# Windowed attention ahead of a SiLU MLP on one core: early transposes ahead of products, V's scale finished inside the MLP, and a ring of four parts for the statistics

## The chip, the cores and the metric

The kernel runs on one core of a Trainium2 chip. The metric is the device time of one execution in microseconds (us). The engines are named as in the profile: PE is TensorE (matmuls; PEld its weight loads), DVE is VectorE, ACT is ScalarE, POOL is GpSimd, SP is SyncE, which here issues every DMA. Each engine works through its own queue in order.

## The reference

```python
def _attn_ref(q, k, v):                       # (8, 8, 576, 64): batch, heads, sequence, width
    scores = scale * np.matmul(q, k.transpose(0, 1, 3, 2))
    bias = slopes[:, None, None] * (-np.abs(rel))[None]
    mask = (rel >= 0) & (rel < 128)           # a causal window of 128
    scores = np.where(mask, scores + bias[None], -1000000000.0)
    attn = np.exp(scores - np.max(scores, axis=-1, keepdims=True))
    attn = attn / (np.sum(attn, axis=-1, keepdims=True) + 1e-09)
    return np.matmul(attn, v)

def _moe_ref(x, w_in, w_out):                 # x: 4608 x 512, w_in: 512 x 2048, w_out: 2048 x 512
    h = x @ w_in
    return (h * (1.0 / (1.0 + np.exp(-h)))) @ w_out
```

The attention's result, heads put side by side, is the x of the MLP. Both run in one launch.

## The kernel before

**Blocks and pairs.** The 4608 rows are 36 blocks of 128 rows. A block has eight heads; four of them are one *pair* p = 2i + q (block i, half q), so there are 72 pairs. Two batches of the reference make one batch b of the kernel: four of them, nine blocks each. The MLP takes groups g of four blocks (512 rows), nine groups, and each group runs 16 slices f of the hidden width; n = 16 g + f counts slices over the whole program.

**An order written out by hand.** Nothing is scheduled by the compiler. The MLP's matmuls are a fixed sequence of *points*, numbered from 0: `gemm1(n, half)` and `gemm2(n, half)`, one half each, 64 points to a group. Everything else is put at a point by `put(point, function, ...)` and is recorded just ahead of that point's matmuls; what stands at the same point keeps the order in which it was put. Points below 0 are the *early part*, which has no matmuls of the MLP: there the attention of the first eight pairs (`p < 2 * GT`) runs alone, in steps of eight points. `at(p)` is the point of pair p's scores: `STEP * (p - 8) - 18` for the first eight, the list `CLOSE` for the next eight, then one every eight points.

**A pair.** `scores` (L431, L424): q times k into two PSUM banks. `row_max` (L453): bias and row maximum, on DVE. `exps` (L463): on ACT. For the first eight pairs `p_transpose_first` (L495) transposes the weights on PE and `p_copy_first` copies them out of PSUM, half 0 on ACT (L504), half 1 on DVE (L502); later pairs go through `p_hi`, `p_lo` (L472, L477) and a DMA transpose (L485). `attend` (L514, L527) is the product with V; `normalize` (L540 to L554) divides, on DVE, and frees the PSUM bank. During the MLP the scores of a pair take both banks of tag "a", one of which is that of the `attend` two pairs earlier, so they wait for that pair's `normalize`. `x_transpose`/`x_low` (L579 to L584) make the first group's x.

**V.** V is split into two 16-bit parts, `v_hi` on POOL (L400) and `v_lo` on DVE (L406), with a power-of-two scale per batch. That scale comes from `vscale_load` (a DMA of one block of V), `vscale_reduce` (its absolute maximum) for each of nine blocks, and `vscale_finish` in three stages: a maximum on DVE (L233), a transpose on PE (L237) with five small instructions on DVE, and a broadcast on PE (L247) with a copy (L249). From batch `QK16 = 2` on, q and k get such statistics too: `qk_load` (L202) fetches q and k of a block, `qk_sum` (L212) sums their absolute values on ACT in place.

**The weights.** They are loaded as raw 64-bit words (`w_load`, L720 and L725) and split by `w_next`: two instructions on ACT (L730, L737), one on DVE (`w_join`, L742), one on ACT (`w_hi`, L752) and one on POOL (`w_lo`, L135). Each of 32 slices is split once, some in the early part, the rest during group 0.

**The MLP's chain.** After `gemm1(n)`: `act1` on ACT (gt, L647), `act2` on DVE (L652), `act3` on ACT (gh, L660 or L662), `act4` (gl; on POOL at L135 in groups 0 to 2 but for the last slice, then on DVE). `gemm2(n)` needs gh for its first two matmuls and gl for the third. At the end of a group `turn_over` does these at once.

**DMA waits.** SP's DMAs use eight semaphores in turn. SP stops at a DMA until what it overwrites is free, and everything behind it in SP's queue stops too.

Of the kernel before, what the change touches and what calls it, by code (L numbers as in the profile page):

```python
# [6 lines left out]
F32 = mybir.dt.float32  # L7
# [5 lines left out]
AF = mybir.ActivationFunctionType  # L13
# [4 lines left out]
P = 128  # L18
B, H, S, D = 8, 8, 576, 64
NHP = H // 2  # L20
DM, DFF = 512, 2048
# [3 lines left out]
NBLK = SB // P  # L25
# [7 lines left out]
GT = TG // P  # L33
NF = DFF // P
NCC = DM // P
# [19 lines left out]

IN16, OUT16 = 2, 3
QK16 = 2
STATS16 = ("w1_10", "w1_11")
RAW16 = ("w1_0", "w1_1")
Q16 = ("w1_2", "w1_3")  # L60
K16 = ("w1_4", "w1_5", "w1_6")
# [9 lines left out]
KEPT = 6  # L71
WD = (1, 2, 3)

CLOSE = (1, 5, 8, 14, 20, 26, 32, 38)


def at(p):

    if p < 2 * GT:
        return STEP * (p - 2 * GT) - 18  # L80
    if p < 4 * GT:
        return CLOSE[p - 2 * GT]
    return STEP * (p - 2 * GT) - LEAD
# [3 lines left out]
def tile_window_attention_then_silu_mlp(ctx, tc, qk, qk16, v, w_in, w_out, base8, out):  # L87
# [35 lines left out]
    def early_tile(i):  # L123
        return early_part(i // 2, i % 2)
# [49 lines left out]

    def vscale_load(b, i):

        t = early_tile(i) if b == 0 else pool.tile([P, DM], F32, tag="rv", bufs=2, name=f"vm{b}_{i}")
        nc.sync.dma_start(t, v[b, i * P : (i + 1) * P, :])
        vred.setdefault(b, {})[i] = t = t.rearrange("p (h d) -> p h d", h=H)
        if b == 0 and i < KEPT:  # L180
            rvs[i] = t

    def vscale_reduce(b, i):
# [6 lines left out]
        else:  # L190
            junk = pool.tile([P, H, D], F32, tag="gt", name=f"vj{b}_{i}")
            nc.scalar.activation(junk, t, AF.Abs, accum_out=m)

    def qk_load(b, i):

        if b == QK16:
            if i == 0:
                vred[b, "qk"] = pool.tile([P, 4, DM], F32, tag="xl", bufs=1, name=f"qs{b}")
            t = vred[b, "qk"][:, 2 * (i % 2) : 2 * (i % 2) + 2]
        else:  # L200
            t = pool.tile([P, 2, DM], F32, tag=STATS16[i % 2], bufs=1, name=f"qs{b}_{i}")
        nc.sync.dma_start(  # L202
            t.rearrange("p k (h c) -> p k h c", h=NHP), qk[b * NBLK + i].rearrange("k p h c -> p k h c")
        )
        vred[b, "qk", i] = t

    def qk_sum(b, i):

        t = vred.pop((b, "qk", i))
        for k in range(2):  # L210
            m = vred[b]["m"][:, (1 + k) * VCH + i : (1 + k) * VCH + i + 1]
            nc.scalar.activation(t[:, k], t[:, k], AF.Abs, accum_out=m)  # L212

    wsc = {}

# [367 lines left out]
    def x_low(cc):  # L583
        nc.vector.tensor_sub(xl[:, cc], xps.pop(cc), f32(xh[:, cc]))  # L584
# [219 lines left out]
    def put(point, fn, *a):  # L804
        plan.setdefault(max(point, at(0)), []).append((fn, a))

    for p in range(NPAIR):
        i, q = divmod(p, 2)
        n = at(p)
        if p < 2 * GT:  # L810
            a = n + 2 * STEP + 1
        elif p == 2 * GT:
            a = n + 10
        elif p == 2 * GT + 1:
            a = n + 12
        else:
            a = n + (15 if p < 4 * GT else 13 if i < QK16 * NBLK else 12)
        if i >= QK16 * NBLK:
            put(n - 18, load_qk16, p)
            put(n - 10, hi16, p, 0)  # L820
            put(n - 8, hi16, p, 1)
            put(n - 6, lo16, p, 0)
            put(n - 5, lo16, p, 1)
            if block_of(i) == 0 and q == 0:
                put(n, rescale_bias, i // NBLK)
        put(n, scores, p)
        if block_of(i) in (SPLIT, SPLIT + 1):
            put(n + 1, other_batch, p)
        put(n + 1, row_max, p, 0)
        put(n + 1, row_max, p, 1)  # L830
        put(n + 2, exps, p, 0)
        put(n + 3, exps, p, 1)
        if p < 2 * GT:

            for u in range(2):
                put(n + STEP + 3, p_transpose_first, p, u)
                put(n + STEP + 4, p_copy_first, p, u)
        else:
            put(n + 3, p_hi, p, 0)
            put(n + 4, p_lo, p, 0)  # L840
            put(n + 4, p_hi, p, 1)
            put(n + 4, p_transpose, p, 0)
            put(n + 5, p_lo, p, 1)
            put(n + 5, p_transpose, p, 1)
        put(a, attend, p)
        z = a + 1
        put(z, normalize, p, 0)
        put(z + 1, normalize, p, 1)
        put(z + 2, x_hi, p)
        put(z + 2, x_lo, p)  # L850
        if q == 0:
            if 1 < i < QK16 * NBLK:
                put(at(2 * i - 3) + 1, load_q, i)
                put(at(2 * i - 3) + 1, load_k, i)
            if i >= KEPT:
                put(n + 4, load_v, i)
            if i == GT:
                put(a - 5, v_hi, i - 1)
                put(a - 4, v_lo, i - 1)
            if i >= GT:  # L860
                put(a - 3, v_hi, i)
                put(a - 2, v_lo, i)
    for k in range(2 * NF):
        put(STATS + k, w_stat, k % 2, k // 2)
    for x, wait in enumerate((0, 2, 5)):
# [3 lines left out]
            for k, fn in enumerate((conv1, conv2, conv3)):  # L869
                put(n + SLICE * f + (CLEAR if f > 4 else 0) + (k if which or f else 0), fn, which, f)  # L870
    for g in range(1, NG):
        put(at(2 * GT * g) + 10, x_unit, g)
        if g >= IN16:
            put(g * SLICE * NF - 2, mlp_scales, g)
    for b in range(1, NBB):

        n = at(2 * GT * (NBLK * b // GT)) + 2
        for i in range(VCH):
            put(n - 53 + 5 * i, vscale_load, b, i)
            put(n - 49 + 5 * i, vscale_reduce, b, i)  # L880
            if b >= QK16:
                put(n - 52 + 5 * i, qk_load, b, i)
                put(n - 46 + 5 * i, qk_sum, b, i)
        for x, wait in enumerate((0, 2, 5)):
            put(n + wait, vscale_finish, b, x)

# [27 lines left out]
    with tc.manual_schedule():  # L914
        make_identity(nc, ident)
        nc.gpsimd.memset(ones, 1.0)
        ps_of("a", "warm")
        keep_warm(16)

        warm = const.tile([P, 1], F32, name="warm")  # L920
        nc.scalar.activation(warm, ones[:, :1], AF.Exp)
        load_q(0)
        load_k(0)
        nc.sync.dma_start(tab[:, :, P:], base8[:, :, P:])
        load_whole(0)
        load_q(1)
        load_k(1)
        nc.sync.dma_start(tab[:, :, :P], base8[:, :, :P])
        load_whole(1)
        nc.gpsimd.memset(v1[:, :, :, D : D + 1], 1.0)  # L930
        for i in (2, 3):
            put(at(2 * i - 3) + 1, load_whole, i)
        for i in range(GT, VCH):
            put(at(4) + 3 + 3 * (i - GT), vscale_load, 0, i)
        for i in range(VCH):
            put(at(3) + 6 + 4 * i, vscale_reduce, 0, i)
        for x in range(3):
            put(at(7) + (6, 8, 16)[x], vscale_finish, 0, x)
        for n in range(AHEAD):
            put(at(1) + 4 + 5 * n, w_next_load)  # L940
        put(at(0) + 1, keep_warm, 6)
        put(at(1) + 1, keep_warm, 16)
        for n in (at(5) + 5, at(6) + 5, at(7) + 5):
            put(n, w_next)
        for cc in range(2):
            put(at(7) + 13 + cc, x_transpose, cc)
        put(at(7) + 14, x_low, 0)
        put(at(7) + 20, x_low, 1)
        while pos[0] < 0:
            begin()  # L950
            pos[0] += 1
        bank.update(scores=[("a", "a")])

        for g in range(NG):
            now[0] = g

            seq = []
            for f in range(NF):
                n = g * NF + f
                seq += [("g1", n, 0)] + [("xt", 0, 2), ("xt", 0, 3)] * (n == 0) + [("g1", n, 1)]  # L960
                if 0 < f < NF - 1:
                    seq += [("g2", n - 1, 0), ("g2", n - 1, 1)]
            n = g * NF + NF - 1
            seq += [("g2", n - 1, 0), ("g2", n - 1, 1), ("g2", n, 0), ("g2", n, 1)]
            for k, n, half in seq:
                if k == "xt":
                    x_transpose(half)
                    x_low(half)
                    continue
                begin()  # L970
                x_send()
                if k == "g1":
                    gemm1(n, half)
                    if half == 1:
                        act1(n)
                        if n % NF == NF - 1:
                            turn_over(n)
                        else:
                            later(1, act2, n)
                            later(2, act3, n)  # L980
                            later(2, act4, n)
                else:
                    gemm2(n, half)
                    if n % NF == NF - 1:
                        store(g, 2 * half)
                        store(g, 2 * half + 1)
                if g == 0 and half == (n == 0):
                    w_next()
                pos[0] += 1
        while plan:  # L990
            begin()
            pos[0] += 1
# [41 lines left out]
```

## Time and profile before

| what | us |
|---|---|
| runs of before: median, lowest, highest (3) | 952.33, 951.69, 953.88 |
| the profiled execution | 949.61 |
| its span in the trace | 947.8 |
| PE busy | 921.9 (97%) |
| DVE, ACT, POOL busy | 655.0, 558.9, 133.5 |

The profiled execution is the one whose trace is read here; 1.8 us of it lie outside the span. Matmuls are pipelined, so PE busy at 97% says that little time is left between matmuls, not that each runs at its best rate. In a row of the timeline stand: start and duration in us, engine, line, operation, output<-input, shape, how many alike were merged, and in square brackets the idle time of that engine just before, with what ended it. In a row of waits: who waited for whom, us in total, how many times, the longest.

### The profile page before, as it was taken

Reading aid. Unit: us, or ns where it says so; the run is one execution under the profiler, and the core shown is the slowest. Engines: PE = TensorE matmul, PEld = TensorE weight load, DVE = VectorE, ACT = ScalarE, POOL = GpSimd, SP = SyncE. Lnnn points to the kernel's source line nnn. Section 1 sums busy time; section 2 is a strip of 40 time slices with the busy share of each in tenths; the row PEclk is TensorE's granted clock in tenths of the full one; section 3 lists DMA queues with packets and bytes.
Section 4 is the critical chain, followed back from the end, with each engine's and each line's share of the span. In section 5 each row is a group of like instructions: output and inputs, shape, how many; then the busy total and the mean of one; then the engine's idle time right before and its main releaser. Section 6 shows DMA issues by size and latency. Waiting matters only on the chain.

```text
span 947.8 us, 17110 instructions
## 1 busy us (share of the span) xinstructions
PE 921.9 (97%) x6442; PEld 574.9 (61%) x6442; DVE 655.0 (69%) x1603; ACT 558.9 (59%) x1152; POOL 133.5 (14%) x122
## 2 busy tenths in 40 slices
PE   8799999999999999999999999999999999999998
PEld 7677777777778888555545555555555545554443
DVE  4687887555778887899687778776777777743222
ACT  5678888676555674666567756555655565532222
POOL 0145665121212221000000000000000000000000
PEclk9999999999999999999999999999999999999999
DMA  9949942423277762644597765544654554421001
GB/s 277 375 119 246 272 101 67 106 65 87 65 181 200 166 142 50 156 101 101 111 244 179 221 144 132 118 112 98 139 111 104 119 142 106 87 55 56 1 1 44
DMA packets 209266, 123.28 MB, mean 130 GB/s; under 512 B 172576, under 2 KB 180768, under 8 KB 209184
## 3 DMA queue, kind: packets, MB, share of 16 engines
q1 hardware_dynamic: 209184, 122.19, 51.9%
q8 instruction: 50, 0.82, 0.4%
q14 instruction: 32, 0.26, 0.1%
HBM read 72.35 MB, written 9.44 MB: 86 GB/s over the span
## 4 chain that ended last, share of the span: by engine, by line
PE 78%; ACT 5%; DVE 5%; issue 2%; DMA 1%; POOL 1%; SPq 0%; DVEq 0%; ACTq 0%; POOLq 0%
PE o L700 34%; PE h L634 29%; PE h L639 6%; PE av L527 4%; PE sp L424 3%; PE sp L431 2%; DVE wm L742 1%; ACT t L463 1%; DVE t L453 1%; DVE gt L652 1%; ACT gt L647 1%; DVE x L137 1%; ACT wr L737 1%; ACT hr L472 1%; DVE v L406 1%
## 5 line engine op out<-in xcount | busy, mean ns | idle before, releaser
L700 PE MATMUL o<-w,gh 128*128 128x512 f16 (+1 forms) x1152 | 351.2, 386 | 1.4 <-ACT gh L660 1.4
L634 PE MATMUL h<-xt,w 128*128 128x512 f16 (+1 forms) x1536 | 310.6, 353 | 0.0
L647 ACT ACTIVATE gt<-h,gsc 128x512 f32<-128x512 f32 x112 | 77.0, 688 | 259.9 <-PE h L634 257.6
L700 PE MATMUL o<-w,gl 128*128 128x512 f16 (+1 forms) x576 | 221.8, 385 | 2.7 <-POOL gl L135 1.5
L634 PEld LDWEIGHTS <-w 128*128 128x128 f16 x1536 | 144.5, 98 | 125.8 <-issue 2.2
L652 DVE SCALAR_TENSOR_TENSOR gt<-gt,h 128x512 f32<-128x512 f32 x144 | 98.6, 685 | 122.6 <-ACT gt L647 122.1
L700 PEld LDWEIGHTS <-gh 128*128 128x128 f16 x768 | 74.8, 98 | 88.7
L463 ACT ACTIVATE t<-t,mx 128x256 f32<-128x256 f32 (+1 forms) x288 | 121.2, 487 | 12.3 <-DVE mx L453 12.1
L477 DVE SCALAR_TENSOR_TENSOR hr<-t,hr 128x512 f16<-128x512 f32 (+1 forms) x128 | 94.6, 741 | 23.5 <-ACT hr L472 23.3
L668 DVE SCALAR_TENSOR_TENSOR gl<-gt,gh 128x512 f16<-128x512 f32 x96 | 66.4, 692 | 53.9 <-ACT gh L662 51.3
L639 PE MATMUL h<-xh,w 128*128 128x512 f32 x256 | 90.0, 405 | 0.0
L400 POOL TENSOR_SCALAR v<-rv,vsc 128x512 f16<-128x512 f32 x30 | 24.4, 814 | 446.1 <-DMA rv<-v 233.1
L135 POOL TENSOR_TENSOR gl<-gt,gh 128x512 fp32r<-128x512 f32 x45 | 60.2, 1337 | 189.0 <-ACT gh L660 154.7
L700 PEld LDWEIGHTS o<-w,gh 128*128 128x128 f32 x384 | 69.9, 188 | 16.6 <-ACT gh L660 1.8
L472 ACT ACTIVATE hr<-t 128x512 f16<-128x512 f32 (+1 forms) x128 | 76.3, 601 | 1.0 <-DMA hl<-hr 1.0
L662 ACT ACTIVATE gh<-gt 128x512 f16<-128x512 f32 x96 | 60.2, 627 | 22.1 <-DVE gt L652 20.9
L700 PEld LDWEIGHTS <-gl 128*128 128x128 f16 x384 | 37.5, 98 | 47.9 <-DVE gl L668 3.5
L527 PEld LDWEIGHTS <-hl 128*128 128x128 f16 x1464 | 51.8, 98 | 22.4 <-issue 13.0
L453 DVE CUSTOM_DVE_ANT_0 t<-sp,tab,vsc 128x256 f32<-128x256 f32 (+1 forms) x144 | 58.6, 463 | 9.2 <-PE sp L424 8.8
L527 PE MATMUL av<-v,hl 128*128 128x65 f16 (+1 forms) x1464 | 55.8, 193 | 7.1 <-DVE v L406 5.7
L137 DVE SCALAR_TENSOR_TENSOR x<-xs,x 128x256 f16<-128x256 f32 x64 | 43.9, 687 | 24.0 <-ACT x L564 23.7
L453 DVE CUSTOM_DVE_ANT_0 t<-sp,tab 128x256 f32<-128x256 f32 (+1 forms) x144 | 50.5, 401 | 13.4 <-DMA tab<-base 7.1
(130 smaller groups left out, 1026.4 us busy)
## 6 DMA issues: line engine op xcount, KB each, us to landing
r<-qk SPq DMA_DIRECT2D x36, 512.0 KB, 4.2
out<-ot SPq DMA_DIRECT2D x36, 256.0 KB, 2.5
qs<-qk SPq DMA_DIRECT2D x18, 512.0 KB, 5.7
wr<-w_in SPq DMA_DIRECT2D x16, 512.0 KB, 7.3
wr<-w_out SPq DMA_DIRECT2D x16, 512.0 KB, 6.8
rv<-v SPq DMA_DIRECT2D x30, 256.0 KB, 3.1
vm<-v SPq DMA_DIRECT2D x27, 256.0 KB, 4.1
q<-qk SPq DMA_DIRECT2D x18, 256.0 KB, 3.6
```

Of the source, the lines that this page charges most:

```text
L135: engine.tensor_sub(out, a, b)
L453: nc.vector.tensor_tensor_reduce(out=t[:, h, 2 * P - n :], in0=st[p]["sp"][h][:, u, o].rearrange("p o c -> p (o c)"), in1=tab[:, 4 * q + 2 ...
L463: nc.scalar.activation(x, x, AF.Exp, bias=st[p]["mx"][:, 2 * u + h : 2 * u + h + 1], scale=-1.0)
L472: nc.scalar.activation(split_of(p, u, hr)[:, 0], t[:, :, 2 * P - n :], AF.Copy, scale=PSCALE)
L477: nc.vector.scalar_tensor_tensor(out=hr[:, 1], in0=t[:, :, 2 * P - n :], scalar=PSCALE, in1=hr[:, 0], op0=ALU.mult, op1=ALU.subtract)
L527: nc.tensor.matmul(av[:, 2 * u + h, : rhs.shape[-1]], lhs, rhs, start=(n == 0), stop=(n == len(seq) - 1), skip_group_check=True,)
L634: nc.tensor.matmul(o, w[:, wp, cc], x, start=start and k == 0, stop=stop, skip_group_check=True)
L639: nc.tensor.matmul(hps[n], w[:, cc], x, start=(half == 0 and i == 0), stop=(half == 1 and i == len(seq) - 1), skip_group_check=True,)
L647: nc.scalar.activation(gt, hps[n], AF.Tanh, scale=scale)
L652: nc.vector.scalar_tensor_tensor(out=gt, in0=gt, scalar=1.0, in1=hps[n], op0=ALU.add, op1=ALU.mult)
L668: nc.vector.scalar_tensor_tensor(out=gl, in0=gt, scalar=CUT, in1=gh, op0=ALU.mult, op1=ALU.subtract)
L700: nc.tensor.matmul(ops[ti], a[:, t], w, start=(f == 0 and i == 0), stop=(f == NF - 1 and i == len(seq) - 1), skip_group_check=True,)
```

## The change

1. In the early part the transposes of a pair are put two points sooner and its product with V two points later (for pair 7: four points sooner), so that in each step PE does scores(p), transposes(p-1), product(p-2) where it did scores(p), product(p-2), transposes(p-1). The copies on ACT (half 0) now stand ahead of the next pair's exponentials.
2. V's scale of batch 0 is finished in the MLP: stage 0 at point -18, stage 1 (transpose) at point 1, stage 2 (broadcast) at point 4. It stood at -20, -18 and -10.
3. All four x transposes stand ahead of point 0; two stood inside the first `gemm1`. Pair 8's scores go to point -6 (`CLOSE[0]`), from 1.
4. Four weight slices instead of three are split ahead of the MLP, one in each step from pair 4 on, and none at point 1. The raw loads start six points later, V's block loads earlier.
5. `v_hi` and `v_lo` stand two points sooner throughout, and V's load three points sooner.
6. The statistics of later batches: for batch 1 the loads follow the list `VM1`. In batch 2, V, q and k of a block are three loads into the four parts of one tile, taken in turn (V of block i in part 3i mod 4, q in 3i + 1, k in 3i + 2); V had tiles of its own, and q and k of a block one 512 KB load into one of two halves. In batch 3 V, q and k have tiles of their own, two of each. The loads of block i stand at point n - 53 + 5i (q and k: one sooner), V's reduction at n - 48 + 5i (one later), the sums at n - 47 + 5i (one sooner).

```diff
-CLOSE = (1, 5, 8, 14, 20, 26, 32, 38)
+CLOSE = (-6, 5, 8, 14, 20, 26, 32, 38)
+VM1 = (-1, 3, 7, 11, 15, 19, 24, 32, 37)
...
-STATS16 = ("w1_10", "w1_11")
+STATS16 = (("w1_10", "w1_11"), ("w1_14", "w1_15"))
...
     def vscale_load(b, i):
-        t = early_tile(i) if b == 0 else pool.tile([P, DM], F32, tag="rv", bufs=2, name=f"vm{b}_{i}")
+        if b == 0:
+            t = early_tile(i)
+        elif b == QK16:
+            t = stat_parts(b)[:, 3 * i % 4]
+        else:
+            tag, bufs = ("rv", 2) if b == 1 else (("w1_12", "w1_13")[i % 2], 1)
+            t = pool.tile([P, DM], F32, tag=tag, bufs=bufs, name=f"vm{b}_{i}")
...
     def qk_load(b, i):
-        if b == QK16:
-            if i == 0:
-                vred[b, "qk"] = pool.tile([P, 4, DM], F32, tag="xl", bufs=1, name=f"qs{b}")
-            t = vred[b, "qk"][:, 2 * (i % 2) : 2 * (i % 2) + 2]
-        else:
-            t = pool.tile([P, 2, DM], F32, tag=STATS16[i % 2], bufs=1, name=f"qs{b}_{i}")
-        nc.sync.dma_start(t.rearrange(...), qk[b * NBLK + i].rearrange("k p h c -> p k h c"))
-        vred[b, "qk", i] = t
+        for k in range(2):
+            if b == QK16:
+                t = stat_parts(b)[:, (3 * i + 1 + k) % 4]
+            else:
+                t = pool.tile([P, DM], F32, tag=STATS16[k][i % 2], bufs=1, name=f"qs{b}_{i}_{k}")
+            nc.sync.dma_start(t.rearrange("p (h c) -> p h c", h=NHP), qk[b * NBLK + i, k])
+            vred[b, "qk", i, k] = t
...
-        if p < 2 * GT:
-            a = n + 2 * STEP + 1
+        if p == 2 * GT - 1:
+            a = n + 13
+        elif p < 2 * GT:
+            a = n + 2 * STEP + 3
         elif p == 2 * GT:
-            a = n + 10
+            a = n + 17
...
-                put(n + STEP + 3, p_transpose_first, p, u)
-                put(n + STEP + 4, p_copy_first, p, u)
+                put(n + STEP + 1, p_transpose_first, p, u)
+                put(n + STEP + 1 + u, p_copy_first, p, u)
...
-                put(n + 4, load_v, i)
+                put(n + 1, load_v, i)
             if i == GT:
-                put(a - 5, v_hi, i - 1)
-                put(a - 4, v_lo, i - 1)
+                put(a - 6, v_hi, i - 1)
+                put(a - 5, v_lo, i - 1)
             if i >= GT:
-                put(a - 3, v_hi, i)
-                put(a - 2, v_lo, i)
+                put(a - 5, v_hi, i)
+                put(a - 4, v_lo, i)
...
-        put(at(2 * GT * g) + 10, x_unit, g)
+        put(max(8, at(2 * GT * g) + 10), x_unit, g)
...
-            put(n - 53 + 5 * i, vscale_load, b, i)
-            put(n - 49 + 5 * i, vscale_reduce, b, i)
+            x = VM1[i] if b == 1 else n - 53 + 5 * i
+            put(x, vscale_load, b, i)
+            put(x + (4 if b == 1 else 5), vscale_reduce, b, i)
             if b >= QK16:
-                put(n - 52 + 5 * i, qk_load, b, i)
-                put(n - 46 + 5 * i, qk_sum, b, i)
+                put(n - 53 + 5 * i, qk_load, b, i)
+                put(n - 47 + 5 * i, qk_sum, b, i)
...
-            put(at(4) + 3 + 3 * (i - GT), vscale_load, 0, i)
+            put(at(2) + 4 + 5 * (i - GT), vscale_load, 0, i)
...
-            put(at(7) + (6, 8, 16)[x], vscale_finish, 0, x)
+            put((-18, 1, 4)[x], vscale_finish, 0, x)
         for n in range(AHEAD):
-            put(at(1) + 4 + 5 * n, w_next_load)
+            put(at(2) + 2 + 5 * n, w_next_load)
...
-        for n in (at(5) + 5, at(6) + 5, at(7) + 5):
-            put(n, w_next)
-        for cc in range(2):
-            put(at(7) + 13 + cc, x_transpose, cc)
-        put(at(7) + 14, x_low, 0)
-        put(at(7) + 20, x_low, 1)
+        for p in range(4, 2 * GT):
+            put(at(p) + 5, w_next)
+        for cc in range(NCC):
+            put(-10 + cc, x_transpose, cc)
+            put(-10 + cc, x_low, cc)
...
-                seq += [("g1", n, 0)] + [("xt", 0, 2), ("xt", 0, 3)] * (n == 0) + [("g1", n, 1)]
+                seq += [("g1", n, 0), ("g1", n, 1)]
...
-                if g == 0 and half == (n == 0):
+                if pos[0] > 0 and g == 0 and half == 0:
                     w_next()
```

What the built programs hold, engine by engine, at three places. In these names a number follows the tile's own name: t5_0 is pair 5's weights, half 0; hl4_0 its copy after the transposes for pair 4; wm, wr and w are a weight slice on its way; vj0_4 is the absolute maximum of V's block 4.

ACT in the early part, the step of pair 6, before:

```order
L463 ACTIVATE t6_0_441<-t6_0_441,mx6_430 128x256 x2
L463 ACTIVATE t6_1_444<-t6_1_444,mx6_430 128x256 x2
L504 COPY hl5_0_467<-pt5_0_455 128x512
L730 ACTIVATE wm1_0_473<-wr1_0_211 128x512
L737 ACTIVATE wr1_0_211<-wr1_0_211 128x512
L192 ACTIVATE vj0_6_476,vmx0_287<-early3_378 128x512
L752 CAST w0_1_481<-wm1_0_473 128x512
```

and after:

```order
L514 COPY hl5_0_444<-pt5_0_439 128x512
L473 ACTIVATE t6_0_451<-t6_0_451,mx6_435 128x256 x2
L473 ACTIVATE t6_1_454<-t6_1_454,mx6_435 128x256 x2
L740 ACTIVATE wm0_1_480<-wr0_1_285 128x512
L747 ACTIVATE wr0_1_285<-wr0_1_285 128x512
L199 ACTIVATE vj0_6_483,vmx0_290<-early3_288 128x512
L762 CAST w1_0_488<-wm0_1_480 128x512
```

Pair 5's copy moved from behind pair 6's exponentials to ahead of them; the rest of the step is the same seven rows, with the third weight slice where the second stood.

SP in group 2, from the first load of batch 2's statistics on (vm2_0 is V of block 0; qs2 is q and k; rv13 is V of block 13 for the product; hl26 is pair 26's DMA transpose), before:

```order
L178 DMA vm2_0_3246<-v 128x512
L713 DMA out<-ot1_2_3254 128x512
L713 DMA out<-ot1_3_3257 128x512
L202 DMA qs2_3263<-qk 128x2x512
L178 DMA vm2_1_3356<-v 128x512
L202 DMA qs2_3263<-qk 128x2x512
L485 DMA_TRANSPOSE hl26_0_3389<-hr26_0_3369 128x8x128
L395 DMA rv13_3391<-v 128x512
L485 DMA_TRANSPOSE hl26_1_3436<-hr26_1_3387 128x8x128
L178 DMA vm2_2_3467<-v 128x512
```

and after:

```order
L185 DMA qs2_3246<-v 128x512
L214 DMA qs2_3246<-qk 128x512 x2
L723 DMA out<-ot1_2_3256 128x512
L723 DMA out<-ot1_3_3259 128x512
L405 DMA rv13_3333<-v 128x512
L185 DMA qs2_3246<-v 128x512
L214 DMA qs2_3246<-qk 128x512 x2
L495 DMA_TRANSPOSE hl26_0_3393<-hr26_0_3372 128x8x128
L495 DMA_TRANSPOSE hl26_1_3436<-hr26_1_3391 128x8x128
L185 DMA qs2_3246<-v 128x512
```

Each block's V, q and k now go out together, all into one tile, and the second block's three stand ahead of pair 26's transposes.

ACT at the same place (gt33, gh33 belong to slice 33 of the MLP, hr26 to pair 26, w16 to the conversion of a weight to 16 bits; the qs2 row is `qk_sum`, two instructions), before:

```order
L463 ACTIVATE t26_1_3330<-t26_1_3330,mx26_3308 128x256 x2
L472 ACTIVATE hr26_0_3369<-t26_0_3327 128x512
L780 ACTIVATE w16_0_3_3371<-w0_6_1080,vscw_2830 128x512
L660 CAST gh33_3374<-gt33_3352 128x512
L472 ACTIVATE hr26_1_3387<-t26_1_3330 128x512
L212 ACTIVATE qs2_3263,vmx2_3334<-qs2_3263 128x512 x2
L647 ACTIVATE gt34_3451<-h34_3397,gsc2_3203 128x512
```

and after:

```order
L473 ACTIVATE t26_1_3330<-t26_1_3330,mx26_3308 128x256 x2
L482 ACTIVATE hr26_0_3372<-t26_0_3327 128x512
L790 ACTIVATE w16_0_3_3374<-w0_6_1083,vscw_2830 128x512
L222 ACTIVATE qs2_3246,vmx2_3356<-qs2_3246 128x512 x2
L670 CAST gh33_3378<-gt33_3352 128x512
L482 ACTIVATE hr26_1_3391<-t26_1_3330 128x512
L657 ACTIVATE gt34_3451<-h34_3397,gsc2_3203 128x512
```

Block 0's two sums moved ahead of gh33. They are recorded at point 133; block 1's three loads at point 132. Since part 3i + 1 of block i's q is also part 3(i+1) + 2 of block i+1's k, the first of the two sums reads a part that the load of block 1's k, recorded ahead of it, writes, and waits for the semaphore of that load. So it is for blocks 0 to 7 of batch 2. In the same way the load of block i+1's q waits for DVE's reduction of V of block i, whose part it takes.

More of the change, by code (lines that the diff above doesn't have):

```diff
@@ L192, in vscale_reduce, with stat_parts @@
             nc.scalar.activation(junk, t, AF.Abs, accum_out=m)
+    def stat_parts(b):
+        if (b, "parts") not in vred:
+            vred[b, "parts"] = pool.tile([P, 4, DM], F32, tag="xl", bufs=1, name=f"qs{b}")
+        return vred[b, "parts"]
     def qk_load(b, i):
-        if b == QK16:
-            if i == 0:
-                vred[b, "qk"] = pool.tile([P, 4, DM], F32, tag="xl", bufs=1, name=f"qs{b}")
-            t = vred[b, "qk"][:, 2 * (i % 2) : 2 * (i % 2) + 2]
-        else:
-            t = pool.tile([P, 2, DM], F32, tag=STATS16[i % 2], bufs=1, name=f"qs{b}_{i}")
-        nc.sync.dma_start(
-            t.rearrange("p k (h c) -> p k h c", h=NHP), qk[b * NBLK + i].rearrange("k p h c -> p k h c")
-        )
-        vred[b, "qk", i] = t
+        for k in range(2):
[5 more added lines that the diff above has]
+            vred[b, "qk", i, k] = t
     def qk_sum(b, i):
-        t = vred.pop((b, "qk", i))
         for k in range(2):
+            t = vred.pop((b, "qk", i, k))
             m = vred[b]["m"][:, (1 + k) * VCH + i : (1 + k) * VCH + i + 1]
-            nc.scalar.activation(t[:, k], t[:, k], AF.Abs, accum_out=m)
+            nc.scalar.activation(t, t, AF.Abs, accum_out=m)
     wsc = {}
@@ L965, in tile_window_attention_then_silu_mlp @@
             for k, n, half in seq:
[L966 to L969, printed above, removed]
                 begin()
```

## The prediction

> **What bounds the kernel now.** I read the page's busy times, then its chain, then what PE waited for.
>
> ```profile
> PE 921.9 (97%) x6442; PEld 574.9 (61%) x6442; DVE 655.0 (69%) x1603; ACT 558.9 (59%) x1152; POOL 133.5 (14%) x122
> ...
> PE 78%; ACT 5%; DVE 5%; issue 2%; DMA 1%; POOL 1%; SPq 0%; DVEq 0%; ACTq 0%; POOLq 0%
> ```
>
> PE is the bound: 97% busy, and 78% of the chain that ended last. The change removes no matmul, so it can win only what PE waits, and a start that is shortened. It loses wherever it makes PE wait. The rows of what PE waited for (total, times, longest) show how little there is to win:
>
> ```profile
> PE av L527 <- DVE v L406: 5.7, 6, 1.3
> PE vt L237 <- DVE vcol L233: 3.6, 1, 3.6
> ...
> PE o L700 <- DVE gl L668: 0.8, 1, 0.8
> ```
>
> **Gain 1: the early part (edits 1 to 4).** The timeline of PE and of ACT's copies from 15 to 57 us:
>
> ```profile
> 15.49 1.16 PE L431 MATMUL sp<-k,q 64*128 64x128 f32 x16
> 21.04 0.56 ACT L504 COPY hl<-pt 128x512 f32<-128x512 f32 x1
> 25.53 0.56 ACT L504 COPY hl<-pt 128x512 f32<-128x512 f32 x1
> 26.15 2.00 PE L514 MATMUL av<-vf,hl 128*128 128x65 f32 x16 [0.52 <-ACT hl L504]
> 27.98 1.04 PE L495 MATMUL pt<-ident,t 128*128 128x128 f32 x8
> 28.96 1.16 PE L431 MATMUL sp<-k,q 64*128 64x128 f32 x16
> 30.13 0.56 ACT L504 COPY hl<-pt 128x512 f32<-128x512 f32 x1
> 37.26 0.27 PE L237 MATMUL vt<-ident,vcol 128*1 128x128 f32 x1 [3.64 <-DVE vcol L233]
> 37.37 2.58 PE L514 MATMUL av<-vf,hl 128*128 128x65 f32 x16
> 39.74 1.91 PE L495 MATMUL pt<-ident,t 128*128 128x128 f32 x8
> 40.84 0.59 ACT L504 COPY hl<-pt 128x512 f32<-128x512 f32 x1 [2.02 <-PE pt L495]
> 41.48 1.61 PE L579 MATMUL xp<-ident,early 128*128 128x128 f32 x8
> 43.33 2.00 PE L514 MATMUL av<-vf,hl 128*128 128x65 f32 x16
> 49.48 0.50 PE L639 MATMUL h<-xh,w 128*128 128x512 f32 x1
> 55.34 0.72 PE L700 MATMUL o<-w,gh 128*128 128x512 f32 x2 [1.41 <-ACT gh L660]
> 56.70 0.50 PE L700 MATMUL o<-w,gl 128*128 128x512 f32 x1 [0.63 <-POOL gl L135]
> ```
>
> In a step with a weight slice ACT's copies stand 4.60 apart (25.53 to 30.13). PE's own work in a step, by starts, is 1.83 (26.15 to 27.98) + 0.98 (to 28.96) + 1.16 = 3.97, so the step is ACT's, and a fourth weight step is not free. What the change gains is position. Pair 3's copy, at 21.04, waited for the exponentials of pair 4; now the transposes follow pair 4's scores and the copy precedes those exponentials. In the timeline, scores at 15.49 are followed by 1.04 of transposes: 15.49 + 1.16 + 1.04 = 17.7 for that copy. Four steps of 4.5 bring pair 7's copy to 35.7; it stood at 40.84. From there to the second half of the first gemm1 it took 8.64 (to 49.48). Of these, 2.49 lay between the copy and its product at 43.33, since the x transposes of 41.48 and V's broadcast stood there; now the product follows the copy's 0.6, so 1.9 less. Behind it the last two x transposes wait for DVE's division, which half a gemm1 covered before: 0.8 more. 35.7 + 8.64 - 1.9 + 0.8 = 43.2 for the second half, against 49.48. Its own tail gets longer: pair 8's row maximum, x_low and the five small instructions of V's scale all stand on DVE ahead of `act2`. I take 8.0 from there to the first gl matmul, an estimate, against 7.22 (49.48 to 56.70): one instruction like DVE's 0.7 more in PE's waits. So 51.2 instead of 56.70: **-5.5**. Ends: -7 if the tail does not lengthen, -3.5 if every weight step takes 5.0.
>
> The 3.64 us wait for V's scale goes with stage 1's move behind gemm1, and with it the slow stretch after it, which the next fence's first row shows as a granted clock of 0.79. (The Trainium skill, "TensorE: Matmul & The Clock Gate", section "Why this matters for your kernels", asks for no PE gap over about 3 us, as the clock halves behind one; the trace agrees: a product of 2.58 behind the gap against 2.00, transposes of 1.91 against 1.04.) This is inside the -5.5.
>
> **Gain 2: V two points sooner (edit 5).** Group 6's last case, in the timeline:
>
> ```profile
> 754.74 0.53 SPq L395 DMA_DIRECT2D rv<-v  x1
> ...
> 758.03 0.70 POOL L400 TENSOR_SCALAR v<-rv,vsc 128x512 f16<-128x512 f32 x1 [22.42 <-DVE sp L444]
> ...
> 763.27 0.74 DVE L406 SCALAR_TENSOR_TENSOR v<-rv,vsc,v 128x512 f16<-128x512 f32 x1
> 764.07 0.76 PE L527 MATMUL av<-v,hl 128*128 128x64 f16 x20 [0.90 <-DVE v L406]
> ```
>
> `v_lo` runs just before the product, behind the gl of a turnover. Two points sooner it stands ahead of the turnover, and V's high part was there at 758.7. All six waits go: **-5.65**. End: -4, if some come back on another instruction of DVE. One PE wait of 0.81 for DVE's gl falls behind a reduction that waited for its DMA; that reduction moves: **-0.8** (end: 0). Gains together -12, at least -9 with tails that lengthen.
>
> **The loss: batch 2's ring (edit 6).** Fetched as three loads into four parts, block i + 1's k lands in the part that held block i's q, and ACT's first sum of block i, recorded one point later, must wait for that landing. That load in turn stands on SP behind the loads of V and q of block i + 1, and q takes the part that DVE's reduction of block i must have read first. So eight times between two blocks ACT stops until a load that has only just been issued lands. Queued on ACT behind the sum are gh, `hr` and the next `act1`, for which POOL, DVE and PE wait. The windows of the early stretch and of batch 2's stretch (span, then busy us of PE, PEld, DVE, ACT, POOL, granted clock, DMA share, GB/s), and the landings between 280 and 350 us (median in the last column) and of k over the whole run:
>
> ```profile
> 36.00:44.00 8.00, 6.64 (x41) 6.00 (x42) 3.73 (x13) 3.39 (x7) 1.27 (x1) 0.79 1.06 390
> 285.40:351.30 65.90, 65.63 (x583) 54.04 (x582) 55.60 (x118) 43.17 (x98) 15.85 (x14) 1.00 0.73 173
> ```
> ```profile
> vm<-v SPq DMA_DIRECT2D x7, 256.0 KB, 3.3
> ...
> k<-qk SPq DMA_DIRECT2D x3, 256.0 KB, 3.6
> ```
> ```profile
> DMA to landing us min/median/max: 3.0/3.7/8.2
> ```
>
> And the first block's place in the timeline:
>
> ```profile
> 282.87 0.67 DVE L189 TENSOR_REDUCE vmx<-vm 128x1 f32<-128x512 f32 x1
> ...
> 284.38 0.60 ACT L660 CAST gh<-gt 128x512 fp32r<-128x512 f32 x1
> ...
> 285.42 0.62 ACT L212 ACTIVATE qs<-qs 128x512 f32<-128x512 f32 x1
> 285.94 0.19 ACT L212 ACTIVATION_READ_ACCUMULATOR qs<-qs 128x1 f32 x1
> ...
> 287.84 0.71 PE L700 MATMUL o<-w,gh 128*128 128x512 f32 x2
> 288.39 0.39 PE L700 MATMUL o<-w,gl 128*128 128x512 f32 x1
> ...
> 300.92 0.69 ACT L647 ACTIVATE gt<-h,gsc 128x512 f32<-128x512 f32 x1 [1.67 <-PE h L634]
> 302.25 0.42 DVE L554 TENSOR_TENSOR xs<-av,r 128x256 f32<-128x256 f32 x1
> 303.54 1.16 PE L431 MATMUL sp<-k,q 64*128 64x128 f32 x16
> ```
>
> On before's time scale: the reduction ends at 283.5, q and k go out at 0.45 each, k at 284.0, and lands 3.5 later at 287.5. ACT is at the sum at 284.4: it stands 3.1. The two sums take 1.3 (0.52 and 0.19 from start to start, twice), so gh starts at 288.8 where it started at 284.38, POOL's gl ends near 290.75, and PE, which took gl at 288.39, is 2.35 late. The next block has little time to recover, as ACT, DVE and then SP's next loads are late together. Walked so for all eight blocks, each with its own rows of the same timeline and a landing of 3.5 to 3.6 (stall of ACT / PE's delay so far): 3.1 / 2.35; 4.05 / 3.25; 4.9 / 7.9; 4.5 / 12.55; 6.05 / 14.6; 3.1 / 18.5; 6.8 / 22.2; 5.2 / 24.4. The third block's step is large because the `act1` of 300.92 and then the xs of 302.25 wait, and pair 28's scores at 303.54 with them.
>
> Bounds: the stalls sum to 37.7. If ACT were never idle otherwise, the stretch would take 43.17 + 37.7 = 80.9 instead of 65.9: +15.0. With landings at their least, 3.0 (0.55 less, eight times: 33.3), +10.6. Above, two PE waits of the walk are 4.65 long, longer than the 3.64 that brought the clock to 0.79; that one cost the next product and transposes 0.58 + 0.87 = 1.45, so twice 2.9: +27.3. I take the walk, **+24.4**, not +15.0, since ACT does idle in these stretches (1.67 at 300.92, for PE) and waits in a ring of engines add up. A clock drop is left to the bound. By a page alone: the Trainium skill, "DMA: Bandwidth & Descriptors", section "Anatomy of one DMA", fits 2.0 us + bytes / 436e3 for its GpSimd path, an estimate of 2.6 for 256 KB; stalls and walk in proportion would then come to +19. The rows here, at 3.0 and more, speak against it.
>
> **At nothing.** Weight slices 4 and on lose one place at point 1, where ACT waited for PE. Batch 3's separate tiles and batch 1's `VM1` move DMAs of 256 KB by a few points past the output's and V's on SP; DVE, at 69%, covers a late reduction; without cover each costs up to one landing, 3.3.
>
> **Sum.** -5.5 - 5.65 - 0.8 + 24.4 = +12.4, on the profiled execution's 949.61: 962.0. The median lies 2.72 above that execution, so **964.7**.
>
> **Rivals.**
> - *The ring's waits are hidden.* PE has matmuls in hand when ACT stops. For it speaks one row, where a sum waited 2.63 for its DMA and PE, in the rows around it, lost nothing:
>
> ```profile
> 489.24 0.63 ACT L212 ACTIVATE qs<-qs 128x512 f32<-128x512 f32 x1 [2.63 <-DMA qs<-qk]
> ```
>
>   With a mean stall of 4.7, the gains of 12 are used up when 1.5 of each shows on PE; so the kernel is faster if over 3.2 of each is hidden. At 4.0 hidden, the loss is 5.6: 952.33 - 12 + 5.6 = 946. Against it: there ACT had no gl and xs behind the sum in the same slice, and one such wait came alone; and 80.9 of ACT in 65.9 cannot hide by itself. Chance 0.17.
> - *Loss and gains balance.* The loss is 10.6 to 14, just ACT's sum with short landings. 951 to 954. Chance 0.09.
> - *The clock drops too.* Two more halts over 3.64: 964.7 + 2.9 = 967.6. For it the 0.79; against it 4.65 rests on a walk. Chance 0.2.
> - *The early part gains nothing*, because four weight steps of ACT push as far as the removed wait pulled: 964.7 + 5.5 = 970.2. Against it stands the copy's new place. Chance 0.08.
>
> **How the numbers follow.** No change, by this kernel's runs, is within 0.2% (1.9 us). The forecast has 0.46, and the two rivals above it 0.28: slower 0.74, same 0.09, faster 0.17. The range goes from the bounds with the most gain and the least loss, 952.33 - 12 + 10.6 = 950.9, put at 950, to the least gain and the most loss, 952.33 - 9 + 27.3 = 970.6, put at 971. The faster cases lie outside it. Among the slower ones alone it is 957 to 971.
>
> **What the next profile would show.** Right: ACT's sum waits for the DMA of k in eight places of group 2, 3 to 7 us each, some 38 in all; PE waits there for gh, gl and scores; the stretch from block 0's sum to block 7's is 20 to 27 longer. Pair 7's copy is near 36 and the first gl matmul near 51; no PE wait for vcol over 1 us; no wait of the product for `v_lo`. Wrong: sums that wait and a stretch of unchanged length (the first rival), or landings near 2.5. The forecast fails at the step from ACT's stall to PE's delay, if anywhere: the stalls follow from the order of loads, but what reaches PE is a walk.

## The result and the profile after

The changed kernel takes 973.86 us (median of 4, 973.49 to 974.67), the one before 953.11 (median of 4): a ratio of 1.0219, interval 1.0200 to 1.0238, so 20.75 us slower. I had forecast slower, 964.7, with a range up to 971: the sign was right, the change of +12.4 was 8 us short of the measured one, and the time lies outside the range. The profiled execution has a span of 971.7 against 947.8.

Busy times and chain on the page of the changed kernel:

```profile
PE 939.4 (97%) x6442; PEld 585.7 (60%) x6442; DVE 653.5 (67%) x1603; ACT 556.1 (57%) x1152; POOL 131.6 (14%) x122
...
PE 72%; DVE 5%; ACT 4%; DMA 2%; issue 2%; POOL 0%; SPq 0%; ACTq 0%; POOLq 0%; DVEq 0%
```

The same 6442 matmuls keep PE busy 17.5 us longer, which points at its clock, and DMA has doubled its share of the chain. What PE waited for, and one row of what ACT waited for:

```profile
PE o L710 <- ACT gh L670: 7.3, 5, 2.9
PE o L710 <- POOL gl L136: 6.7, 10, 1.2
PE sp L441 <- DVE xs L564: 6.6, 4, 3.8
...
PE sp L441 <- DVE vsc L259: 1.5, 1, 1.5
...
PE pt L505 <- ACT t L473: 1.2, 1, 1.2
```
```profile
ACT qs L222 <- DMA qs<-qk: 35.9, 8, 7.7
```

ACT's sums wait eight times, 35.9 us in all; the walk had eight and 37.7. The waits for V (5.7), for vcol (3.6) and for DVE's gl (0.8) are gone from PE's rows. In their place stand gh, gl and xs, as the walk had it. Block 0 of batch 2 in the timeline:

```profile
283.27 0.67 DVE L196 TENSOR_REDUCE vmx<-qs 128x1 f32<-128x512 f32 x1
...
283.96 0.80 SPq L214 DMA_DIRECT2D qs<-qk  x2
...
288.19 0.63 ACT L222 ACTIVATE qs<-qs 128x512 f32<-128x512 f32 x1 [3.33 <-DMA qs<-qk]
...
289.44 0.60 ACT L670 CAST gh<-gt 128x512 fp32r<-128x512 f32 x1
290.09 0.73 PE L710 MATMUL o<-w,gh 128*128 128x512 f32 x2 [1.62 <-ACT gh L670]
...
291.45 0.74 PE L710 MATMUL o<-w,gl 128*128 128x512 f32 x1 [0.62 <-POOL gl L136]
```

The load goes out when the reduction has ended, the sum stands 3.33 (walk: 3.1), gh comes behind it, and PE is 1.62 + 0.62 late (walk: 2.35).

Where the time went can be read by matching the first matmul of each slice's gemm2 in the two timelines, after minus before: -3.45 at slice 0, +1.47 at slice 1, +0.40 at slice 32, +28.55 at slice 44, +23.80 at the end. So the start gained nothing, batch 2's stretch lost 28.2, and the later groups gained 4.7. The windows of that stretch, slices 32 to 44, in the kernel before and in the changed one:

```profile
280.77:359.35 78.58, 77.67 (x675) 63.61 (x673) 67.83 (x149) 51.12 (x114) 19.77 (x16) 1.00 0.70 169
```
```profile
281.17:387.91 106.74, 89.63 (x676) 69.12 (x673) 67.52 (x149) 51.10 (x114) 19.76 (x16) 0.92 0.47 129
```

The same instructions on every engine: ACT's 51.1 us of work are unchanged. PE is idle 17.1 instead of 0.9, and its granted clock is 0.92 instead of 1.00, which costs 0.08 x 106.74 = 8.5, an estimate. PE's busy time grew by 12.0; what the other 3.4 are, the trace does not show. In the whole run the clock was halved 34 us instead of 3.4.

The start, in the timeline of the changed kernel:

```profile
28.85 1.90 PE L524 MATMUL av<-vf,hl 128*128 128x65 f32 x16
31.94 1.94 PE L505 MATMUL pt<-ident,t 128*128 128x128 f32 x8 [1.19 <-ACT t L473]
33.68 6.92 PE L524 MATMUL av<-vf,hl 128*128 128x65 f32 x32
40.40 2.88 PE L589 MATMUL xp<-ident,early 128*128 128x128 f32 x16
...
53.24 0.50 PE L710 MATMUL o<-w,gl 128*128 128x512 f32 x1 [0.62 <-POOL gl L136]
...
56.35 2.07 PE L441 MATMUL sp<-k,q 64*128 64x128 f32 x14 [1.50 <-DVE vsc L259]
58.36 1.22 PE L710 MATMUL o<-w,gh 128*128 128x512 f32 x2
```

Pair 7's copy is where I put it (35.55), but the two products behind it take 6.92 instead of 3.8: the clock is halved from 32.1 to 42.4. And at 56.35 pair 9's scores wait for V's scale, whose copy stood on DVE behind a reduction that waited for batch 1's first load of V. That load, at point -1, is behind pair 8's two DMA transposes on SP:

```profile
49.16 2.71 SPq L495 DMA_TRANSPOSE hl<-hr  x2
51.92 1.04 SPq L185 DMA_DIRECT2D vm<-v  x2
```
```profile
54.95 0.69 DVE L196 TENSOR_REDUCE vmx<-vm 128x1 f32<-128x512 f32 x1 [3.76 <-DMA vm<-v]
...
56.15 0.15 DVE L259 COPY vsc<-vs 128x2 f32<-128x2 f32 x1
```

### The profile page after: what moved, and what is told of

It is laid out like the page before. It is cut to its first block, busy times and chain, and to the rows that moved or that the text cites. A ratio compares the mean times of both kernels' runs of the same rounds, so it can differ in the third digit from the quotient of the medians.

```text
span 971.7 us, 17160 instructions
## 1 busy us (share of the span) xinstructions
PE 939.4 (97%) x6442; PEld 585.7 (60%) x6442; DVE 653.5 (67%) x1603; ACT 556.1 (57%) x1152; POOL 131.6 (14%) x122
## 4 chain that ended last, share of the span: by engine, by line
PE 72%; DVE 5%; ACT 4%; DMA 2%; issue 2%; POOL 0%; SPq 0%; ACTq 0%; POOLq 0%; DVEq 0%
PE o L710 32%; PE h L644 26%; PE h L649 5%; PE av L537 4%; PE sp L434 3%; DMA qs<-qk 2%; PE sp L441 2%; ACT qs L222 1%; DVE hr L487 1%; ACT t L473 1%; DVE gt L662 1%; ACT gh L670 1%; DVE wr L796 1%; DVE w L802 1%; DVE t L463 0%
## 5 line engine op out<-in xcount | busy, mean ns | idle before, releaser
L644 PE MATMUL h<-xt,w 128*128 128x512 f16 (+1 forms) x1536 | 313.8, 356 | 0.0
L710 PE MATMUL o<-w,gl 128*128 128x512 f16 (+1 forms) x576 | 224.4, 390 | 6.7 <-POOL gl L136 6.7
L710 PEld LDWEIGHTS o<-w,gh 128*128 128x128 f32 x384 | 71.9, 194 | 24.8 <-ACT gh L670 9.7
L138 DVE SCALAR_TENSOR_TENSOR x<-xs,x 128x256 f16<-128x256 f32 x64 | 43.1, 673 | 33.4 <-ACT x L574 33.2
L441 PE MATMUL sp<-k,q 64*128 64x128 f32 x544 | 47.7, 296 | 8.7 <-DVE xs L564 6.6
```

What stands on the lines that cost most here:

```text
L441: nc.tensor.matmul(sp[h][:, u, o], qs[i][rows, 2 * q + u], ks[i - 1 + o][rows, 2 * q + u], start=True, stop=True, skip_group_check=True,)
L644: nc.tensor.matmul(o, w[:, wp, cc], x, start=start and k == 0, stop=stop, skip_group_check=True)
L710: nc.tensor.matmul(ops[ti], a[:, t], w, start=(f == 0 and i == 0), stop=(f == NF - 1 and i == len(seq) - 1), skip_group_check=True,)
```

## The experiments

Each is compared with runs of the kernel before on the same chip; a kernel's own median and the ratio with its interval are given.

**What in batch 2 costs the time.** Three runs. First, the changed kernel with the sums one point sooner, ahead of the next block's loads:

```diff
-                put(n - 47 + 5 * i, qk_sum, b, i)
+                put(n - (48 if b == QK16 else 47) + 5 * i, qk_sum, b, i)
```

> The changed kernel with one edit: in batch 2 the sums of block i are recorded one point sooner, ahead of block i + 1's loads. The ring of four parts, the loads and their points stay. Theory: the 28 us that the changed kernel loses between the MLP's slices 32 and 44 come from ACT's sum waiting for the next block's load, so ACT's 35.9 us of waits for the DMA of qs fall under 6 and the time to 973.9 - 28 = 946 (943 to 950). Rival: the ring itself loses the time, since three loads per block stand closer on SP and crowd out the transposes; then the waits move to SP and the time stays above 962.

Second, the ring taken out of the changed kernel, with V in tiles of tag "rv", q and k in one load, and the points of before:

```diff
-        elif b == QK16:
-            t = stat_parts(b)[:, 3 * i % 4]
...
-                t = stat_parts(b)[:, (3 * i + 1 + k) % 4]
+            t = stat_parts(b)[:, 2 * (i % 2) : 2 * (i % 2) + 2]
...
```

> The changed kernel with batch 2's statistics as before the change: V in tiles of its own, q and k of a block in one load of 512 KB into one of two halves, at the points of before. Theory: as without the ring's waits, 946 (943 to 950), and within 2 us of the kernel that only records the sums sooner. Rival (the loss is partly in something else of group 2, such as V two points sooner on POOL and DVE): 952 or more.

Third, the kernel before with the ring's loads, parts and points of the change's diff, and nothing else of it:

> The kernel before with nothing but batch 2's ring of four parts and its points. Theory: the whole loss of the ring, 953.1 + 28 = 981 (977 to 985), with ACT waiting some 36 us in eight places for the DMA of qs and the clock halved in several stretches of group 2. Rival (my walk was right on this kernel, and V two points sooner made it worse in the changed one): 953.1 + 24.4 = 977.5 or less.

Measured: 944.21 (0.9897, 0.9870 to 0.9923), 944.48 (0.9906, 0.9888 to 0.9924) and 981.01 (1.0293, 1.0268 to 1.0318). With the sums one point sooner, what ACT waited for has one small row of this kind left; with the ring alone there are nine waits, eight of them in batch 2 (38.5 us):

```profile
ACT qs L222 <- DMA qs<-qk: 0.4, 1, 0.4
```
```profile
ACT qs L226 <- DMA qs<-qk: 39.9, 9, 8.0
```

All three came as the theory said. The ring with its loads may stay; only ACT's order against them matters. The order also decides what is summed. In the changed kernel the first sum of blocks 0 to 7 is recorded behind the load that puts the next block's k into the same part, so by the order of the program it adds up that k in place of the block's own q; recorded one point sooner it adds up q. What this does to the result no run here measured. One point in a table of numbers turns 1.022 into 0.990. The rival (SP's traffic) falls.

**The early part and V, each alone.** Both put lines of the change's diff, and no others, into the kernel before: edits 1 to 4, and edit 5.

> The kernel before with edits 1 to 4 alone (transposes ahead of products, V's scale finished inside the MLP, x whole, four slices). Batch 1's loads stay where they were. Theory: the early part's order is shorter by 8 us, but gives 5 back to a halved clock from pair 7's transposes on; no late load of batch 1 here, so 953.1 - 3.5 = 949.6 (948 to 951.5). Rival (the start gains as I predicted, and what spoiled it is batch 1's list): 947.5 or less. Second rival (the start gains nothing in itself): 953.

> The kernel before with edit 5 alone: V's load three points sooner, both parts of V two points sooner. Theory: the six waits of the product for DVE's part of V go, 5.7 us in all, and nothing takes their place: 953.1 - 5.2 = 947.9 (946.5 to 949.5). Rival: DVE's instruction displaces gl or act2 where it now stands, and half is given back: 950 or more.

Measured: 952.83 (0.9996, 0.9982 to 1.0010) and 950.63 (0.9988, 0.9976 to 1.0001). Neither gains what I had priced at 5.5 and 5.65. Of the early part's ten runs nine have a granted clock of 0.989 to 0.992 over the whole run, against 0.995 or 0.996 in most runs of before; the tenth, at 0.999, took 949.28. 0.004 of 950 us is 3.8 us, an estimate: in size, what the shorter start gained goes to a slower clock. Its trace, matched slice by slice, is 3.24 sooner than before at slice 0 and 0.90 later at slice 1. Between them lie a halved stretch from 54.5 to 61.3 and the same wait for batch 1's first load of V as in the changed kernel:

```profile
49.37 2.71 SPq L485 DMA_TRANSPOSE hl<-hr  x2
...
52.13 0.58 SPq L178 DMA_DIRECT2D vm<-v  x1
...
55.17 0.69 DVE L189 TENSOR_REDUCE vmx<-vm 128x1 f32<-128x512 f32 x1 [3.77 <-DMA vm<-v]
```

I had expected no late load here, since this kernel does not have the list `VM1`. So the list is not what makes it late: pair 8's earlier scores (edit 3) put that pair's two DMA transposes ahead of it on SP. The first of the next two runs moves the load ahead of them, and the wait goes.

With V alone, the waits for V are gone from PE's rows, and groups 3 to 8 gain 3.5. But groups 0 and 1 lose 3.0 between slices 3 and 17; there PE waits for `xs`, gh and gl instead. In the timeline of that kernel, which before had 0.76 at this place:

```profile
124.73 1.13 PE L431 MATMUL sp<-k,q 64*128 64x128 f32 x14 [1.52 <-DVE xs L554]
```

A halved window from 126.4 to 129.9 follows it. That V's instruction is what made `xs` late was not tried by itself.

**Batch 1's first load, and the gap ahead of pair 7's transposes.**

```diff
-            put(x, vscale_load, b, i)
+            put(x if x >= 0 else -8, vscale_load, b, i)
```

> The changed kernel with the first load of batch 1's V at point -8 instead of -1, ahead of pair 8's two transposes on SP; its reduction stays. Theory: DVE's 3.76 us wait for that load, behind which V's scale, a weight's join and act2 stood, goes, and with it PE's 1.5 us wait at 56 us and the half clock from 56 to 62.8: 4.9 us lost between slices 0 and 1, so 973.9 - 4.5 = 969.4 (968 to 971). Rival: another instruction of DVE or the product of pair 8 is late in its place, 972 or more.

```diff
+        put(-18, keep_warm, 10)
```

> The changed kernel with ten more idle matmuls of 252 columns (their result is not read) ahead of pair 7's transposes, where PE waits 1.19 us. Theory: this gap made the clock halve from 32.1 to 42.4 us; filled, the clock stays at full and the products of pairs 6 and 7 take 1.9 each instead of 3.4: 973.9 - 4.5 = 969.4 (968 to 971). Rival: products of 65 columns behind one another keep the clock low by themselves, filled gap or not: 973 to 975.

Measured: 972.00 (1.0219, 1.0200 to 1.0238) and 972.36 (1.0215, 1.0200 to 1.0230), neither resolved from the change's own 1.0219. The first removed its wait in the trace (the reduction at 51.35 instead of 54.95, and 1.8 us lost between slices 0 and 1 instead of 4.9), but a total that the clock moves by some us does not show it. The second did not do what it was for: `keep_warm` writes to the bank of pair 5's product, and had to wait for its division, 2.98 us, so it widened the gap that it was to fill. Its trace speaks against the mechanism of its rival all the same, since there both products, back to back, ran at full clock:

```profile
36.95 3.68 PE L524 MATMUL av<-vf,hl 128*128 128x65 f32 x32
```

> The changed kernel with three edits together: sums recorded ahead of the next block's loads, batch 1's first load of V at point -8, ten idle matmuls ahead of pair 7's transposes. Theory: the three losses add up, 973.9 - 28 - 4.5 - 4.5 = 937 (934 to 942). Rival (they overlap, since a start that is earlier meets another bound in group 0): 943 to 947.

This kernel has all three edits: 943.00 (0.9914, 0.9890 to 0.9938). The ring's loss goes; beside the run with the sums alone (0.9897) no gain of the other two is resolved, and the idle matmuls wait 2.98 us here too. The 937 that I expected was missed.

**The start again, with a free bank.** On a base with the two edits that did in the traces what they were for (sums ahead, first load of V at -8):

> The changed kernel with two edits: the sums ahead of the next block's loads, and batch 1's first load of V at point -8. Theory: the loss of the ring (28 us) and what the late load of V cost (1.9 us as run alone) add up: 944.2 - 1.9 = 942.3 (940.5 to 944). Rival (the start's halved clock swallows the second): 944 or more.

`fill` is written like `keep_warm`, but into a new tile of tag "w":

```diff
+        put(-18, fill, 10)
```

> The two edits above, and ten idle matmuls of 252 columns ahead of pair 7's transposes, this time into a free bank of PSUM (in the earlier try they shared the bank of a product and waited 2.98 us for DVE). Theory A: the 1.19 us in which PE waits there bring the clock down; filled, the mean half-clock time per run falls from some 14 us to 7 and the time by 3.5, to 938.8. Theory B: products of 65 columns in a row do not count as full activity, so the clock falls or stays down in any case: no change beyond 1 us, 942.3.

```diff
+        elif p == 2 * GT - 2:
+            a = n + 16
```

> The two edits above, and pair 6's product ahead of pair 7's transposes, so that the products of pairs 6 and 7 are no longer back to back. Theory B: with transposes between them the halved clock ends after one window of 3.4 us, as in the kernel before, instead of three: 942.3 - 3 = 939.3. Theory A: the wait ahead of the transposes is filled with pair 6's product as far as its copies allow, and the wait for pair 7's copy comes in its place: 942 to 943.5.

Measured: 939.74 (0.9885, 0.9859 to 0.9911), 941.74 (0.9893, 0.9880 to 0.9906) and 942.20 (0.9903, 0.9888 to 0.9918). The base is 0.8 under the range that I gave for it, but its ratio is not resolved from that of the sums alone, 0.9897. It falls into two kinds of execution: three at 936.9 to 937.9 with a granted clock of 1.000, three at 941.6 to 943.8 with 0.990 to 0.993. It is one program; the profiled execution, at 936.92, has no halved stretch but in its last 1.2 us. With the first gap filled there is a halved stretch from 36.6 to 43.4, behind the next wait of 0.86 (for pair 7's copy), where the changed kernel had one from 32.1: filling one gap did not remove it. Products no longer back to back (the third) were halved all the same, 33.4 to 43.6: theory B in that form falls.

The last run on this fills both gaps.

```diff
+        put(-18, fill, 10)
+        put(-14, fill, 9)
```

> The changed kernel with the sums ahead, the first load of V sooner, and idle matmuls in both gaps of PE at the end of the early part: ten ahead of pair 7's transposes, nine ahead of its product (0.86 us). Theory A (idle time brings the clock down): no halved window between 28 and 45 us, a granted clock of 0.996 or more in most runs and 938.5. Theory B (products of 65 columns count as low activity): halved windows stay, 941.5 or more.

Measured: 939.12 (0.9861, 0.9836 to 0.9885), four runs between 936.81 and 939.84. The windows from 28 to 45 us, with one gap filled and with both:

```profile
28.00:45.00 17.00, 16.00 (x113) 14.32 (x110) 10.88 (x32) 10.21 (x22) 2.53 (x2) 0.80 1.03 369
```
```profile
28.00:45.00 17.00, 16.86 (x133) 14.57 (x134) 12.24 (x41) 11.71 (x27) 2.55 (x2) 1.00 1.03 373
```

PE idle 0.14 instead of 1.00, clock 1.00 instead of 0.80: this fits theory A, that the waits bring the clock down, but does not show it, since the unfilled base also ran this stretch at 1.00 in its profiled execution, with 2.08 us idle. With both gaps filled all four runs have a granted clock of 0.996 or more, in the base three of six: perhaps fewer runs at a lower clock, but these are few runs, on another chip. The best time is not lower (936.81 against 936.92). It has the lowest median here, 13.9 per thousand under the kernel before, but is not resolved from the base.

**Where the parts that don't add up lie.** Ring +28, early part 0, V -1 and the rest of edit 6 should be the change's +21.

> The kernel before with edit 6 but for batch 2's ring: batch 1's loads by the list VM1, batch 3's V, q and k in tiles of their own at the new points. The parts run alone so far (ring +28, early part 0, V -1.0) leave 5.5 us of gain of the changed kernel unexplained. Theory: they are here, through waits of PE for DVE's gl behind a reduction that waits for its load (0.8 to 2.8 us in three profiles) and the turnovers of groups 5 to 8: 952 - 3.5 = 948.5. Rival: they are in the parts together (V sooner needs VM1's loads out of its way), then 951 to 952.5 here.

This puts `VM1` and batch 3's tiles into the kernel before: 953.05 (1.0008, 0.9992 to 1.0024), so nothing by itself. With the list but the old early part, the reduction of batch 1's first V waits for no load:

```profile
54.98 0.68 DVE L194 TENSOR_REDUCE vmx<-vm 128x1 f32<-128x512 f32 x1
```

Then V with each of its neighbours:

> The kernel before with edits 1 to 5, edit 6 left out. Theory (V's gain needs the early part, since a start that is shifted lets its instructions fall beside others in groups 0 and 1): 952 - 8 = 944, as the changed kernel with its ring taken out. Rival (V's gain needs the new places of the loads): 950 to 952, the sum of the two alone.

> The kernel before with edit 5 and with edit 6 but for batch 2's ring; the early part as before. Theory (V's gain needs the early part): 951, the sum of the two alone. Rival (batch 1's and 3's loads at their new places are what lets V's gain through): 946 or less.

Measured: 949.06 (0.9966, 0.9950 to 0.9981) and 947.73 (0.9954, 0.9936 to 0.9973). V with the rest of edit 6 gains 4.6, where the two alone come to 0; V with the early part gains 3.2, where the two alone come to 1.0. So V gains more beside other edits than alone. That the loads' places do more for it than the early part is not resolved, since the two intervals overlap. Neither theory was right alone. What exactly they clear for `v_lo` in groups 0 and 1 stays open.

## Why the prediction was wrong in size

By its own steps:

- **The ring** was the right mechanism at the right place: eight waits, 35.9 us (forecast 37.7). The loss was 28.2 in the trace, and 981.01 - 952.87 = 28.1 alone; the walk gave 24.4. Mis-sized were two terms of opposite sign. Without the clock the stretch lost 28.2 - 8.5 = 19.7, under the walk's 24.4 and over the 15.0 of ACT's sum. The clock lost 8.5, where I had 2.9 and kept it out of the sum. I counted only waits longer than 3.64 as able to halve the clock. One such came (3.80, for xs, at 312.6); the other three halvings of the stretch followed shorter ones, in windows with 1.8 to 2.5 us of PE idle (below).
- **The early part** was priced at -5.5 and gave nothing. Pair 7's copy came at 35.55 (35.7 forecast), so the walk through the order was right up to there. Two steps behind it failed. The first took the slow stretch after the wait for vcol as gone with that wait. (Its clock of 0.79 stands in the prediction's fence of windows, under the ring.) In the changed kernel a stretch of three windows (10.24 us, against 3.41 before) follows a wait of 1.19, and the first gl matmul came at 53.24 instead of 51.2. What brings the stretch on stays open: the base has such waits too, and three of its six runs show a clock of 1.000. The second let the sum end at the first gl matmul and put nothing behind it. Pair 8's scores at -6 (edit 3) set its DMA transposes ahead of batch 1's first load of V; DVE waited 3.76 for it, the clock was halved from 56.0 to 62.8, and 4.9 were lost between slices 0 and 1. I had looked for such a wait in `VM1`, at nothing; but the early part without the list has it (3.77) and loses 4.1 there, and the list without the early part does not have it.
- **V**: -5.65 was the sum of waits, as if nothing took their place. Alone it gave 1.0, with the rest of edit 6 4.6. In the changed kernel the later groups gave 4.7, with gl's wait in it.
- **The sum**: all edits but the ring were forecast at -12.0 and measured 944.48 - 952.87 = -8.4; the ring was forecast at 24.4, and measured 973.86 - 944.48 = 29.4 as the last edit. 3.6 + 5.0 = 8.6 is the miss, but for the spread of the runs.
- **The rivals**: the first (waits hidden) fell; its break-even asked for over 3.2 of each wait hidden; of a mean of 4.5 about 2.0 was, since the stretch lost 19.7 / 8 = 2.5 for each without the clock (3.5 with it). The second did not come. The third, the clock, came, at three times its price. The fourth, an early part that gains nothing, came too, by another way than its text. The two together are what the range lacked: it held either one, not both. At their prices they give 964.7 + 2.9 + 5.5 = 973.1; that this is near 973.86 is luck, since the walk was 4.7 too dear and the clock 5.6 too cheap.

## What to carry to other kernels

When a ring of buffers is refilled, look at which engine is recorded first, the reader or the next load: a reader recorded one step late waits for data it doesn't want, in the queue of an engine that others need. Removed waits are worth their sum only where nothing else stands due in the same place, so a part measured alone says little about the part among others. And where PE is the bound, price a wait twice: its own length, and the window of halved clock that may follow.

## What was not expected of the hardware

Every halved stretch in these traces, but for one that the end of a run cuts off, is a whole number of windows of 3.41 us: 13.65, 10.24, 6.83 or 3.41, as here in the changed kernel:

```profile
32.12:42.36 10.24, 10.24 (x50) 9.85 (x50) 4.60 (x15) 4.40 (x11) 1.50 (x2) 0.50 1.06 378
```

PE is busy in all of it, at half the clock. The Trainium skill, "TensorE: Matmul & The Clock Gate", section "What's actually happening", has a free-running window of 4096 cycles, 3413 ns; the traces agree, and the two kinds of execution of one program fit a window that starts anywhere. The rule of the Trainium skill on gaps over about 3 us, in the same page's section "Why this matters for your kernels", which I had leaned on, is not enough here. Taking PE's idle time in each such window of the 17 traces, a window at full clock ahead of a halved one held 0.80 to 3.37 us idle; with over 2.0 the next was always halved (17 times), between 0.8 and 2.0 sometimes. The three with under 1.0 all lie in the early part, among products of 65 columns. Why three full windows of PE work, 32.1 to 42.4, were needed there before the clock rose, when one was enough at 291 us, no run settled.
